# Attention into a gated mixture of experts: the gate's first choice made for all batches from mean values, one logits run per batch, and the value matmuls of two tiles in smaller pieces

## The chip, the cores and the metric

One core of one Trainium2 chip. The metric is device microseconds of the whole program, the median of a few executions. A profile, taken in a further execution, gives the times of single instructions. Engines in the profile's short names: PE (TensorE matmuls), PEld (its weight loads), DVE (VectorE), ACT (ScalarE), POOL (GpSimd), SP (SyncE, which here only issues DMAs).

## What is computed

Multi-query attention feeds a two-level gate, which sends each token to one of 16 experts. Sizes: 8 batches, 16 heads, 384 positions, head width 64; so 3072 tokens of width 1024; 4 groups of 4 experts, each expert two 1024x1024 matrices.

```python
scores = matmul(q, k.T) / 8                    # one k and one v per batch for all 16 heads
attn   = exp(scores - max) / sum
x      = matmul(attn, v)                       # tokens: 3072 x 1024
g_idx  = argmax(x @ w_group)                   # group of a token, weight g_w from a softmax
e_idx  = argmax(x @ w_expert[g_idx])           # expert in the group, weight e_w from a softmax
out    = g_w * e_w * (relu(x @ w1[g, e]) @ w2[g, e])
```

With inputs of scale 0.1 the scores are close to zero, so a token's attention is close to an even mean of its batch's values. The inputs are one fixed draw. In it all 384 tokens of each of batches 0 to 6 go to one expert; in batch 7, 363 go to expert 0 and 21 to expert 2.

## The kernel before

**Tiles, units, steps.** A tile `t` is 128 query positions of a batch `b` (24 tiles, three to a batch). A tile has 8 units; a unit is two heads. The main loop `for i in range(NSL)` (L794) has 96 steps of two units, so tile `t` has steps 4t to 4t+3, and a batch has 12 steps. `p = i % 4` is the step's place in its tile. The order of work is written out by hand: in each step the engines get, in this order,

1. `scores` (L198, matmul L206) of both units: PE writes them into PSUM, which has room for two units, so a unit's scores wait until ACT has read those of the unit two before;
2. `soft` (L212): DVE takes row maxima (L217), ACT the exponentials with row sums (L220, two of 128x384 for a unit);
3. for `p` of 0 or 1, PE work called by `advance` (an expert's matmuls, L479 and L493, in groups of eight) and transposed queries (`q_group`, L183 with ACT's copy L187; from tile 5 on `q_blocks` on DVE, L195); for `p` of 2 or 3, `pv` (L246, matmul L257): half of the value matmuls of the tile before;
4. `transp` (L239): DVE transposes the probabilities of the two units of two steps before into the buffer `ring` (L241), which `pv` reads; `ring` has three slots of four units, and a tile takes two;
5. `norm` (L229): DVE's reciprocal of the sums (L231), then POOL scales the four probability blocks (L235);
6. `pv_out` (L263) after the second half of `pv`: ACT copies four banks (L271), POOL casts to bf16 (L272).

Everything else is hung on a step and a place by `at(step, place, function)` (L721), and `run` calls it there: "m0", "m1", "m3" lie around `advance`; "v" and "m2" behind the PE work and ahead of `transp`; "w" ahead of `norm`; "e" right behind `norm`; "g" at the step's end. Each engine works through its own instructions in that order. A semaphore wait in one holds all that is behind it on that engine.

**The gate before.** The logits of a batch come in two runs: of its first tile at step 12b+8 (`logits`, L280, 32 columns) and of the other two at 12b+16 (64 columns); DVE transposes them (`logits_out`, L290). From the first run, at step 12b+9, `gate_first` (L302 to L306), a small matmul that counts choices over the tile's tokens (`gate_choose`, L341) and `gate_score`, `gate_pick` (L350 to L383) name the batch's main expert; `gate_picked` (L360) makes its one-hot row. `load_main` reads the index into a register of POOL and issues four DMAs of 1 MB from POOL's queue (L454), at step 12b+9, place "g". From step 12b+17 the expert's 14 groups of matmuls are spread over the next batch's steps. Batch 7 has a second expert for the few other tokens; what is left over after that would go through a loop at the end (L911), once for each pair of batch and expert.

**Keys of the next batch.** `load_k` (step 12b+2), `scale_k` on POOL (L167, step 12b+7, "g") and `k_blocks` on DVE (L171, step 12b+8, "e").

In steps 0 to 16 there is no expert to work on, since that of batch 0 begins in step 17.

Of the kernel before, what the change touches and what calls it, by code (L numbers as in the profile page):

```python
# [12 lines left out]
P = 128  # L13
# [6 lines left out]
def kernel(  # L20
# [242 lines left out]
    def pv_out(t):  # L263
        b, j = t // ST, t % ST
        if j < 2:
            st["xt", b, j] = pool.tile([P, KO, ST - 1 if j else 1, P], FP32, tag=f"xt{j}", name="xt", bufs=1)
        xt = st["xt", b, min(j, 1)][:, :, max(j - 1, 0), :]
        if j == 0:
            st["xb", b] = pool.tile([P, KO, S], BF16, tag="xb", name="xb", bufs=2)
        for i, o in enumerate(st.pop(("o", t))):  # L270
            nc.scalar.copy(out=xt[:, :, ts(i, 32)], in_=o[:, 0:2 * P].rearrange("p (c q) -> p c q", c=KO))  # L271
        nc.gpsimd.tensor_copy(out=st["xb", b][:, :, ts(j, P)], in_=xt)  # L272

    def logits(b, j0, j1):

        xt = st.pop(("xt", b, j0))
        lt_ps = xbank()
        for ko in range(KO):
            for c in range(4):
                nc.tensor.matmul(  # L280
                    out=lt_ps[ts(c, 32), 0:32 * (j1 - j0)].rearrange("e (j q) -> e j q", q=32),
                    lhsT=wge[:, ko, :], rhs=xt[:, ko, :, ts(c, 32)],
                    start=(ko == 0), stop=(ko == KO - 1), tile_position=(0, c * 32),
                )
        st["lt_ps", b, j0] = lt_ps
# [60 lines left out]

    def gate_score(b):
# [6 lines left out]

    def gate_pick(b):
        st["smx", b], st["idx", b] = pick(st["scr", b], 0)

    def gate_picked(b):
        ohs = ohs_all[:, ts(b, GE)]
        nc.vector.tensor_scalar(  # L360
            out=ohs, in0=st["scr", b][:], scalar1=st["smx", b][:, 0:1], scalar2=None, op0=ALU.is_equal
        )
        st["ohs", b] = [ohs]
# [95 lines left out]
    def load_main(b, n):  # L459
        if n == 0:  # L460
            st["e", b] = nc.gpsimd.value_load(st.pop(("idx", b))[0:1, 0:1], min_val=0, max_val=GE - 1)
        st.setdefault(("w", b), []).append(load_w(st["e", b], n))
# [267 lines left out]

    for b in range(B):
        s0 = SB * b
        for x, j0, j1 in ((s0 + 8, 0, 1), (s0 + 16, 1, ST)):
            at(x, "m2", logits, b, j0, j1)
            at(x + 1, "m0" if b and j0 == 0 else "v", logits_out, b, j0, j1)
# [16 lines left out]
        if b == B - 1:  # L752
            at(s0 + 13, "w", gate_pick_second, b)
# [5 lines left out]
    for t in range(NT):  # L759
        for x, u, half in ((4 * t, t, 1), (4 * t + 1, t + 1, 0)):  # L760
# [4 lines left out]
        if t < NT - 2:  # L765
            at(4 * t, "g", load_q, t + 2)
# [18 lines left out]
    for e in range(GE):  # L785
        nc.vector.memset(tie16[:, e:e + 1], float(GE - 1 - e))

# [5 lines left out]
    load_v(0)  # L793
    for i in range(NSL):  # L794
# [4 lines left out]
        for u in us:  # L799
            scores(u)  # L800
# [10 lines left out]
        elif t > 0:  # L811
            pv(t - 1, (p - 2) * NB // 2, (p - 1) * NB // 2)
# [8 lines left out]
        if p == 3 and t > 0:  # L821
            pv_out(t - 1)
# [12 lines left out]
    run(i + 1, "w")  # L835
    advance(1)
    load_second(0)
# [124 lines left out]
```

## Time and profile before

| | |
|---|---|
| median of 3 runs | 508.92 us (508.62 to 509.27) |
| the profiled execution's own time | 508.39 us |
| its span in the profile | 507.0 us |
| granted TensorE clock, mean | 0.997 |
| PE busy, share of the span | 481.5 us, 95% |
| DVE busy | 413.0 us, 81% |
| ACT busy | 321.8 us, 63% |
| POOL busy | 289.6 us, 57% |

Rows of a group give line, engine, operation, output<-input with its shapes, and xcount, then busy time in all and the mean of one in ns, then the engine's idle time ahead of them with what ended it. Rows of the timeline give start, duration, engine, line, with the number of instructions merged in xN and, in brackets, the idle time ahead and what ended it. An fp32 matmul is two rows on PE. Matmul ends are modelled, so the distance from one start to the next is the better measure of PE.

### The profile page before, as it was taken

The page shows a single profiled execution, that of the slowest core. Times are in us where ns is not written, and L with a number is a line of the kernel's source. Part 1 is how long each engine was busy: PE and PEld are TensorE (multiplying, and loading weights), DVE is VectorE, ACT ScalarE, POOL GpSimd, SP SyncE. Part 2 cuts the span into 40 slices and gives each one's busy share as a digit, 9 for nine tenths or more (in the row PEclk, how much of TensorE's full clock was granted, in tenths as well). Part 3 has the DMA queues.
Part 4 walks back from the last instruction along what each step waited for, and adds up shares of the span by engine and source line. Part 5 has one row for each costly group of instructions (what it writes and reads, how often), then busy time and mean ns, then how long its engine had stood idle before and what let it go on. Part 6 is the DMA issues. An engine that isn't in the chain of part 4 may idle for free.

```text
span 507.0 us, 20054 instructions
## 1 busy us (share of the span) xinstructions
PE 481.5 (95%) x8256; PEld 262.1 (52%) x8273; DVE 413.0 (81%) x737; ACT 321.8 (63%) x1002; POOL 289.6 (57%) x524
## 2 busy tenths in 40 slices
PE   7597789999999999999999999999999999999994
PEld 3143356555456455555465455555455455555653
DVE  3889979988899879988899879998799888890630
ACT  4776766677676766676676776676775775753421
POOL 1665955684576664584576654584476654584300
PEclk9999999999999999999999999999999999999998
DMA  7612997399947998389946998389956993089993
GB/s 106 145 26 45 174 239 193 76 160 233 255 86 129 220 237 218 75 157 232 261 84 123 217 243 223 75 143 230 245 116 111 210 241 110 1 155 241 231 243 121
DMA packets 64524, 84.04 MB, mean 166 GB/s; under 512 B 20379, under 2 KB 39963, under 8 KB 64432
## 3 DMA queue, kind: packets, MB, share of 16 engines
q0 software_dynamic: 19152, 37.84, 41.3%
q1 hardware_dynamic: 44320, 44.61, 35.2%
q8 instruction: 66, 1.08, 0.9%
q10 hardware_dynamic: 960, 0.30, 0.3%
q14 instruction: 26, 0.21, 0.1%
HBM read 101.52 MB, written 19.40 MB: 239 GB/s over the span
## 4 chain that ended last, share of the span: by engine, by line
PE 90%; DVE 5%; ACT 3%; issue 1%; POOL 0%; POOLq 0%; ACTq 0%; DVEq 0%
PE x L257 26%; PE s L206 25%; PE x L479 15%; PE x L493 13%; PE sb L493 4%; PE x L280 3%; ACT pr L220 3%; DVE nmx L217 2%; PE sb L479 2%; DVE ring L241 2%; PE x L674 1%; PE x L100 1%; PE x L689 1%; PE x L145 0%; PE x L643 0%
## 5 line engine op out<-in xcount | busy, mean ns | idle before, releaser
L235 POOL TENSOR_SCALAR pr<-pr,rinv 128x384 f32<-128x384 f32 x384 | 218.3, 588 | 146.0 <-DVE rinv L231 133.2
L220 ACT ACTIVATE pr<-s,nmx 128x384 f32<-128x384 f32 x384 | 218.0, 579 | 131.5 <-DVE nmx L217 120.0
L217 DVE TENSOR_REDUCE nmx<-s 128x2 f32<-128x768 f32 x192 | 174.3, 948 | 45.7 <-PE s L206 44.6
L241 DVE STREAM_TRANSPOSE ring<-pr 128x768 f32<-128x768 f32 x192 | 175.4, 952 | 0.1
L206 PE MATMUL s<-kt,qt 64*64 64x384 f32 x1536 | 148.9, 496 | 13.3 <-ACT pr L220 12.3
L257 PE MATMUL x<-ring,v_sb 32*64 32x256 f32 x4608 | 137.7, 378 | 0.2
L257 PEld LDWEIGHTS x<-ring,v_sb 32*64 32x64 f32 x4608 | 101.6, 131 | 43.0 <-issue 23.2
L206 PEld LDWEIGHTS s<-kt,qt 64*64 64x64 f32 x1536 | 48.5, 132 | 82.6 <-ACT pr L220 44.4
L220 ACT ACTIVATION_READ_ACCUMULATOR pr<-s,nmx 128x1 f32 x384 | 77.9, 203 | 0.0
L479 PE MATMUL x<-xb,w 128*128 128x384 bf16 x448 | 76.6, 326 | 0.0
L479 PEld LDWEIGHTS <-w 128*128 128x128 bf16 x512 | 47.7, 98 | 42.2 <-issue 12.6
L493 PE MATMUL x<-w,h_t 128*128 128x512 bf16 x276 | 64.7, 380 | 0.6
L493 PEld LDWEIGHTS <-h_t 128*128 128x128 bf16 x384 | 35.7, 98 | 52.0 <-issue 11.9
L454 POOL DMA_DIRECT2D w<-in_moe_w_dram x36 | 27.9, 784 | 10.8 <-issue 9.0
L271 ACT COPY xt<-x 128x256 f32<-128x256 f32 x96 | 28.9, 385 | 2.8 <-PE x L257 2.7
L485 ACT ACTIVATE h_t<-x 128x384 bf16<-128x384 f32 x56 | 25.4, 502 | 6.4 <-PE x L479 6.4
L272 POOL CAST xb<-xt 128x1024 bf16<-128x1024 f32 x24 | 24.9, 1036 | 3.6 <-ACT xt L271 3.6
L511 ACT ACTIVATE y<-x,gsel 128x512 f32<-128x512 f32 x36 | 24.8, 693 | 3.1 <-PE x L493 3.1
L195 DVE STREAM_TRANSPOSE qt<-q_sb 128x512 f32<-128x512 f32 x38 | 26.1, 687 | 0.0
L493 PE MATMUL sb<-w,h_t 128*128 128x512 bf16 x92 | 21.2, 379 | 0.2
L231 DVE RECIPROCAL rinv<-ssum 128x4 f32<-128x4 f32 x96 | 13.9, 144 | 3.3 <-ACT pr L220 3.3
L511 ACT ACTIVATE y<-sb,gsel 128x512 f32<-128x512 f32 x9 | 6.2, 688 | 16.1 <-PE sb L493 16.1
(132 smaller groups left out, 165.6 us busy)
## 6 DMA issues: line engine op xcount, KB each, us to landing
w<-in_moe_w_dram POOLq DMA_DIRECT2D x36, 1024.0 KB, 19.6
q_sb<-in_q_dram SPq DMA_DIRECT2D x76, 224.0 KB, 6.0
out_dram<-y SPq DMA_DIRECT2D x96, 128.0 KB, 6.3
xb_scratch<-xb SPq DMA_DIRECT2D x8, 768.0 KB, 4.3
v_sb<-in_v_dram SPq DMA_DIRECT2D x32, 96.0 KB, 4.0
kk<-in_k_dram SPq DMA_DIRECT2D x28, 92.0 KB, 4.1
q_sb<-in_q_dram SPq DMA_DIRECT2D x16, 128.0 KB, 3.3
q_sb<-in_q_dram SPq DMA_DIRECT2D x5, 64.0 KB, 3.1
```

Of the source, the lines that this page charges most:

```text
L195: nc.vector.transpose(out=qt[:].rearrange("p (x d) -> p x d", d=32), in_=q_sb[:, :, 0:32])
L206: nc.tensor.matmul(out=s[m * D:(m + 1) * D, h, 0:S], lhsT=qt[r, ts(2 * cc + m, D)], rhs=kt[r, :], start=True, stop=True, tile_position=(h ...
L217: nc.vector.tensor_reduce(out=nmx[:], in_=s[:, :, 0:S], axis=AX.X, op=ALU.max, negate=True)
L220: nc.scalar.activation(out=pr[:, h, :], in_=s[:, h, 0:S], func=ACTF.Exp, bias=nmx[:, h:h + 1], scale=1.0, accum_out=ssum[:, k, h:h + 1],)
L235: nc.gpsimd.tensor_scalar(out=pr, in0=pr, scalar1=rinv[:, k, h:h + 1], scalar2=1.0, op0=ALU.mult, op1=ALU.mult)
L241: nc.vector.transpose(out=ring[:, (u // 4) % 3, u % 4].rearrange("p h s -> p (h s)"), in_=st.pop(("pr", u))[:].rearrange("p h s -> p (h s)"),)
L257: nc.tensor.matmul(out=o[i][h * D:(h + 1) * D, 0:2 * P].rearrange("d (g c q) -> d g c q", g=2, c=4), lhsT=v_sb[r, n, :], rhs=ring[r, a:z + ...
L271: nc.scalar.copy(out=xt[:, :, ts(i, 32)], in_=o[:, 0:2 * P].rearrange("p (c q) -> p c q", c=KO))
L454: nc.gpsimd.dma_start(out=w[:, o:o + 4, :], in_=(w1f, w2f)[n][ds(e, 1), :, o:o + 4, :].rearrange("o p c f -> (o p) c f"))
L479: nc.tensor.matmul(out=hp[:, 0:S], lhsT=w1[:, ko, ts(fc, P)], rhs=xb[:, ko, :], start=(ko == 0), stop=(ko == KO - 1))
L493: nc.tensor.matmul(out=yp, lhsT=h_t[:, fo, ts(j, P)], rhs=w2[:, fo, ts(nh, 512)], start=(fo == 0), stop=(fo == FO - 1),)
L511: nc.scalar.activation(out=y[:, ts(nh, 512)], in_=yp, func=ACTF.Copy, scale=g)
```

## The change

For the first choice of the gate the kernel no longer looks at a batch's first tile. It loads the values of all batches once more, sums them over positions (three rows of a partition on POOL in `guess_sum`, over partitions by a matmul with a column of ones in `guess_mean`), takes the logits of the eight sums (`guess_logits`), picks an expert for each batch on DVE and POOL (`guess_pick`), spreads the one-hot rows to all partitions by a matmul (`guess_all`) and makes eight indices (`guess_index`). All of this lies in steps 2 to 5. The buffers are the third slot of `ring`, which the transposes first write in step 6. Batches 0 to 6 then have one logits run, of 96 columns, at step 12b+16. Batch 7 keeps its two runs and its count, for the second expert. Weights of batch 0 are issued in step 7, those of batch 7 in steps 85 and 90, those of the second expert from step 95. `pv` of tiles 0 and 1 is cut into five pieces over three steps; the second place in a step for such a piece is "u", between the scores of the step's two units. `q_group` and `load_q` of tiles 1 to 3 move by one step.

```diff
-        if j < 2:
-            st["xt", b, j] = pool.tile([P, KO, ST - 1 if j else 1, P], FP32, tag=f"xt{j}", name="xt", bufs=1)
-        xt = st["xt", b, min(j, 1)][:, :, max(j - 1, 0), :]
+        if j == 0:
+            st["xt", b] = pool.tile([P, KO, ST, P], FP32, tag="xt", name="xt", bufs=1)
+        xt = st["xt", b][:, :, j, :]
...
+    def guess_load():
+        vs = ring[:, 2, 0:2].rearrange("p u h s -> p (u h s)").rearrange("p (b c d) -> p b c d", b=B, d=D)
+        nc.sync.dma_start(
+            out=vs.rearrange("p b c d -> p b (c d)"), in_=v.rearrange("b o (p c) d -> p (b o) (c d)", c=ST)
+        )
+        st["vs"] = vs
+
+    def guess_sum():
...
+        for part, n in zip(total, (0, B // 2)):
+            part = part[:, 0:B // 2, :]
+            nc.gpsimd.tensor_tensor(out=part, in0=vs[:, n:n + B // 2, 0, :], in1=vs[:, n:n + B // 2, 1, :], op=ALU.add)
+            nc.gpsimd.tensor_tensor(out=part, in0=part, in1=vs[:, n:n + B // 2, 2, :], op=ALU.add)
+            st["total"].append(part)
+
+    def guess_mean():
...
+        for b in range(B):
+            for h in range(2):
+                nc.tensor.matmul(
+                    out=bank[ts(h, D), b:b + 1], lhsT=total[b // (B // 2)][:, b % (B // 2), :], rhs=ident1[:],
+                    start=True, stop=True, tile_position=(0, h * D),
+                )
+        mean = early["mean"]
+        nc.scalar.copy(out=mean, in_=bank[:, 0:B])
...
+    def guess_logits():
...
+        for ko in range(KO):
+            nc.tensor.matmul(
+                out=bank[0:B, 0:NL], lhsT=mean, rhs=wge[:, ko, 0:NL], start=(ko == 0), stop=(ko == KO - 1)
+            )
+        lg = early["lg"][0:B].rearrange("b (g e) -> b g e", e=4)
+        nc.scalar.copy(out=early["lg"][0:B], in_=bank[0:B, 0:NL])
...
+    def guess_pick():
...
+        gp = nc.gpsimd
+        nc.vector.tensor_reduce(out=mx[0], in_=lg, axis=AX.X, op=ALU.max)
+        gp.tensor_tensor(out=lg, in0=lg, in1=mx[0].unsqueeze(2).to_broadcast([B, 1 + G, 4]), op=ALU.subtract)
+        nc.vector.scalar_tensor_tensor(
+            out=lg, in0=lg, scalar=0.0, in1=w4[0:B, 0:1 + G, :], op0=ALU.is_ge, op1=ALU.mult
+        )
+        nc.vector.tensor_reduce(out=mx[1], in_=lg, axis=AX.X, op=ALU.max)
+        nc.vector.tensor_tensor(
+            out=oh, in0=lg, in1=mx[1].unsqueeze(2).to_broadcast([B, 1 + G, 4]), op=ALU.is_equal
+        )
+        gp.tensor_tensor(
+            out=pair, in0=oh[:, 1:1 + G, :], in1=oh[:, 0, :].unsqueeze(2).to_broadcast([B, G, Eg]), op=ALU.mult
+        )
+        gp.tensor_tensor(
+            out=spread, in0=pair.rearrange("b g e -> b (g e)").unsqueeze(1).to_broadcast([B, B, GE]),
+            in1=ident[0:B, 0:B].unsqueeze(2).to_broadcast([B, B, GE]), op=ALU.mult,
+        )
...
+    def guess_all():
...
+        nc.tensor.matmul(
+            out=bank[:, 0:NP], lhsT=early["ones"][0:B], rhs=spread.rearrange("b c e -> b (c e)"), start=True, stop=True
+        )
+        nc.scalar.copy(out=ohs_all[:], in_=bank[:, 0:NP])
...
+    def guess_index():
+        nc.gpsimd.tensor_tensor(
+            out=numbered, in0=ohs_all[:].rearrange("p (b e) -> p b e", e=GE),
+            in1=tie16[:].unsqueeze(1).to_broadcast([P, B, GE]), op=ALU.mult,
+        )
+        number = early["number"]
+        nc.vector.tensor_reduce(out=number, in_=numbered, axis=AX.X, op=ALU.add)
...
+        nc.vector.tensor_scalar(
+            out=idx[:], in0=number, scalar1=-1.0, scalar2=float(GE - 1), op0=ALU.mult, op1=ALU.add
+        )
...
+    for x, where, fn in (
+        (2, "e", guess_sum), (3, "m2", guess_mean), (4, "m2", guess_logits), (4, "e", guess_pick),
+        (5, "m2", guess_all), (5, "e", guess_index),
+    ):
+        at(x, where, fn)
     for b in range(B):
         s0 = SB * b
-        for x, j0, j1 in ((s0 + 8, 0, 1), (s0 + 16, 1, ST)):
+        for x, j0, j1 in ((s0 + 8, 0, 1), (s0 + 16, 1, ST)) if b == B - 1 else ((s0 + 16, 0, ST),):
             at(x, "m2", logits, b, j0, j1)
...
-        at(s0 + 9, "m0" if b else "v", gate_first, b)
-        at(s0 + 9, "m3" if b else "m2", gate_choose, b)
-        at(s0 + 9, "w", gate_score, b)
-        at(s0 + 9, "w", gate_pick, b)
-        at(s0 + (13 if b == B - 1 else 12), "w", gate_picked, b)
         if b == B - 1:
-            at(s0 + 9, "w", load_main, b, 0)
-            at(s0 + 10, "w", load_main, b, 1)
+            at(s0 + 9, "m0", gate_first, b)
+            at(s0 + 9, "m3", gate_choose, b)
+            at(s0 + 9, "w", gate_score, b)
+            at(s0 + 10, "w", gate_pick_second, b)
+            at(s0 + 1, "g", load_main, b, 0)
+            at(s0 + 6, "g", load_main, b, 1)
+            at(s0 + 11, "g", load_second, 0)
         else:
-            at(s0 + 9, "g", load_main, b, 0)
-            at(s0 + 9, "g", load_main, b, 1)
+            at(s0 + (9 if b else 7), "g", load_main, b, 0)
+            at(s0 + (9 if b else 7), "g", load_main, b, 1)
             at(s0 + 16, "g", keep_xb, b)
...
     for t in range(NT):
-        for x, u, half in ((4 * t, t, 1), (4 * t + 1, t + 1, 0)):
+        spread = 0 < t <= ST
+        for x, u, half in ((4 * t + spread, t, 1), (4 * t + 1, t + 1, 0)):
...
         if t < NT - 2:
-            at(4 * t, "g", load_q, t + 2)
+            at(4 * t + spread, "g", load_q, t + 2)
+        x, n0 = 4 * t + 4, 0
+        for p, where, n1 in (
+            ((2, "p", 4), (3, "u", 6), (3, "p", 8), (4, "u", 10), (4, "p", NB)) if t < ST - 1 else
+            ((2, "p", NB // 2), (3, "p", NB)) if t < NT - 1 else ()
+        ):
+            at(x + p, where, pv, t, n0, n1)
...
     load_v(0)
+    guess_load()
     for i in range(NSL):
...
-        for u in us:
-            scores(u)
+        scores(us[0])
+        run(i, "u")
+        scores(us[1])
...
-        elif t > 0:
-            pv(t - 1, (p - 2) * NB // 2, (p - 1) * NB // 2)
+        run(i, "p")
...
-    run(i + 1, "w")
     advance(1)
-    load_second(0)
     few_ready()
```

`scale_k(1)` is still called at place "g" of step 7, behind the four weight DMAs of batch 0, which are now called there too.

More of the change, by code (lines that the diff above doesn't have):

```diff
@@ L765 @@
         if t < NT - 2:
[L766 removed]
+            at(4 * t + spread, "g", load_q, t + 2)
[5 more added lines that the diff above has]
+            at(x + p, where, pv, t, n0, n1)
+            n0 = n1
+            if n1 == NB:
+                at(x + p, "o", pv_out, t)
     load_k_first()
@@ L786 @@
         nc.vector.memset(tie16[:, e:e + 1], float(GE - 1 - e))
+    ident1 = singles.tile([P, 1], FP32)
+    nc.vector.memset(ident1[:], 1.0)
+    early, early_at = {}, 0
+    for name, width in (
+        ("number", B), ("mean", B), ("lg", NL), ("oh", NL), ("pair", GE), ("mx", 1 + G), ("sm", 1 + G),
+        ("ones", P), ("spread", NP), ("numbered", NP),
+    ):
+        early[name] = ring[:, 2, 3].rearrange("p h s -> p (h s)")[:, early_at:early_at + width]
+        early_at += width
+    nc.vector.memset(early["ones"], 1.0)
+    numbered = early["numbered"].rearrange("p (b e) -> p b e", e=GE)
     busy(5)
@@ L820 @@
         run(i, "e")
-        if p == 3 and t > 0:
-            pv_out(t - 1)
+        run(i, "o")
         run(i, "g")
```

37 lines of the change are left out of this document (24 added, 13 removed).

## Prediction

> **What bounds the kernel now.** I read the page's 40 slices first, then busy time by stage (the windows view), the chain that ended last, and the timeline of the first 76 us step by step.
>
> ```profile
> PE   7597789999999999999999999999999999999994
> DVE  3889979988899879988899879998799888890630
> ```
>
> PE fills every slice from the eighth on; in the first six or seven (12.7 us each) it does not, and DVE is as busy as PE there.
>
> ```profile
> 28.00:62.00 34.00, 28.00 (x605) 14.78 (x601) 31.52 (x53) 24.14 (x81) 23.85 (x40) 1.00 0.39 74
> 62.00:75.00 13.00, 11.54 (x304) 7.04 (x300) 10.29 (x14) 8.21 (x29) 7.79 (x13) 1.00 1.12 237
> ...
> 135.00:435.00 300.00, 299.47 (x5298) 162.43 (x5307) 266.18 (x449) 204.05 (x648) 183.09 (x322) 1.00 0.80 173
> ```
> ```profile
> by line: PE s L206 30.6%; PE x L257 29.4%; PE x L479 19.4%; PE x L493 17.6%; PE x L280 2.9%; issue 0.2%; PE x L341 0.0%
> ```
>
> In the windows the columns are PE, PEld, DVE, ACT, POOL, clock, DMA share, GB/s. From 28 to 62 us DVE is busy for 31.5 of 34 us; from 135 to 435 us PE for 299.5 of 300. The last line is the chain from 75 to 435 us: PE alone. So there are two stages. From step 17 (about 75 us) on only PE work taken away or added counts; a wait on POOL or DVE is covered there. Before step 17 each us that DVE loses is lost for good, since PE has nothing to fetch forward. I mark steps by the start of their first L217:
>
> ```profile
> 21.70 1.82 DVE L217 TENSOR_REDUCE nmx<-s 128x2 f32<-128x768 f32 x2
> ...
> 23.44 1.83 DVE L241 STREAM_TRANSPOSE ring<-pr 128x768 f32<-128x768 f32 x2
> ...
> 25.19 0.14 DVE L231 RECIPROCAL rinv<-ssum 128x4 f32<-128x4 f32 x1
> 25.25 1.80 DVE L217 TENSOR_REDUCE nmx<-s 128x2 f32<-128x768 f32 x2
> 25.42 2.27 POOL L235 TENSOR_SCALAR pr<-pr,rinv 128x384 f32<-128x384 f32 x4 [1.27 <-DVE rinv L231]
> ...
> 28.81 1.83 DVE L217 TENSOR_REDUCE nmx<-s 128x2 f32<-128x768 f32 x2
> ```
>
> Steps 4, 5 and 6 begin at 21.70, 25.25 and 28.81. A step is two maxima, two transposes and a reciprocal back to back, 3.55 us: the floor of a step in this stage. POOL scales a step's blocks from 0.23 us behind the reciprocal to 2.5 us behind it.
>
> **The change part by part.** What is added lies in steps 2 to 8, in the stage without cover, and at four places an engine that others need waits for POOL, whose queue has something ahead of what is waited for.
>
> (1) The sums and the mean (steps 2 and 3).
>
> ```profile
> 18.36 2.27 POOL L235 TENSOR_SCALAR pr<-pr,rinv 128x384 f32<-128x384 f32 x4 [1.28 <-DVE rinv L231]
> ...
> 20.50 0.88 PE L206 MATMUL s<-kt,qt 64*64 64x384 f32 x8 [1.61 <-ACT pr L220]
> ```
> ```profile
> L437 POOL TENSOR_TENSOR grem_all<-gate,gs 128x48 f32<-128x48 f32 x8 | 2.3, 289 | 0.6
> L421 POOL TENSOR_TENSOR gw<-wt 128x12 f32<-128x12 f32 x8 | 1.7, 211 | 6.7 <-DVE wt L418 6.7
> L145 PE MATMUL x<-ident,kk 128*64 128x128 f32 x12 | 1.5, 428 | 0.1
> ```
>
> POOL's scaling of step 2 ends at 20.63; the four sums of 128x256 stand behind it. Two-input operations take 211 ns for 12 columns and 289 for 48, 2.2 ns a column, so about 735 ns for 256: 2.9 us for four, to 23.5. The load of the values (0.79 MB, issued at about 12.7) should not be later:
>
> ```profile
> 10.00:20.00 10.00, 5.83 (x52) 1.66 (x52) 7.38 (x12) 7.53 (x25) 6.19 (x11) 1.00 0.94 172
> ```
>
> At the 172 GB/s of that window it takes 4.6 us, to 17.3, and as much again behind other loads would still be 22. [...] `guess_mean` waits for the sums on PE, and behind it in PE's queue are the scores of step 4, at 20.50 before. Half its 32 rows follow the second sum; at between 0.02 us a row and the 0.12 of L145 (1.5 us for 12 rows) they take 0.4 to 2; I take 1.0, since one column moves and not 128. The scores of step 4 then start at 24.5, their first unit is there 0.95 later, and step 4 begins at 25.4 instead of 21.70: **+3.7** (2.0 to 5.5, the low end with sums at half the price).
>
> (2) `guess_pick`, step 4, "e".
>
> ```profile
> L302 DVE TENSOR_REDUCE mx<-lg 128x5 f32<-128x20 f32 x8 | 1.4, 176 | 0.3
> L879 DVE TENSOR_REDUCE fcol<-end 128x1 f32<-128x128 f32 x1 | 0.3, 286 | 0.0
> ```
>
> DVE's second instruction waits for POOL's subtraction, and that stands behind POOL's scaling of step 4, which begins only with the reciprocal. So DVE stands still until 2.5 us behind the reciprocal, plus 0.2 for the subtraction, plus three more small operations at 0.2 with their hand-over, before the maxima of step 5: 3.4 us. `guess_logits` and ACT's two small copies are hidden under the exponentials. `guess_all` waits on PE for POOL, until some 1 us into step 5, when PE has nothing to do: nothing. **+3.4** (2.8 to 4.0).
>
> (3) `guess_index`, step 5, "e". The same again: the product of 128x128 on POOL (0.46 by the slope above) stands behind the scaling of step 5, then DVE reduces (0.29, as L879) and makes the index (0.2): 2.5 + 0.46 + 0.5. **+3.5** (2.8 to 4.2).
>
> (4) The weights of batch 0, now in step 7.
>
> ```profile
> 36.98 2.27 POOL L235 TENSOR_SCALAR pr<-pr,rinv 128x384 f32<-128x384 f32 x4 [2.17 <-DVE rinv L231]
> ...
> 40.21 0.51 POOL L167 TENSOR_SCALAR kk<-kk 128x384 f32<-128x384 f32 x1
> ...
> 41.14 0.58 DVE L171 STREAM_TRANSPOSE kt<-kk 128x384 f32<-128x384 f32 x1
> ...
> 50.50 3.24 POOL L454 DMA_DIRECT2D w<-in_moe_w_dram  x4 [1.48 <-issue]
> ```
>
> The four DMAs hold POOL for 3.24 us, with 1.48 ahead of the first. In step 9 of before nobody waited for POOL. Now `scale_k` (0.51) is behind them, and `k_blocks` waits for it on DVE one step later. Behind the reciprocal of step 7: 2.5 + 1.5 + 3.2 + 0.5 = 7.7 us; `k_blocks` would begin at 3.55 + 0.15 = 3.7. DVE waits 4.0 to 4.2, and the maxima of step 9 are behind it. **+4.1** (2.6 without the 1.48, to 4.5). POOL's own scaling is 4 us late here, but is needed two steps later: hidden.
>
> (5) Steps 6 to 13: what the pieces and the gate give.
>
> ```profile
> 33.26 1.82 DVE L217 TENSOR_REDUCE nmx<-s 128x2 f32<-128x768 f32 x2 [0.82 <-PE s L206]
> ...
> 44.23 0.17 PE L341 MATMUL x<-first,ones 128*128 128x16 bf16 x1 [1.81 <-DVE first L306]
> ...
> 61.82 1.82 DVE L217 TENSOR_REDUCE nmx<-s 128x2 f32<-128x768 f32 x2
> 66.61 1.52 PE L206 MATMUL s<-kt,qt 64*64 64x384 f32 x15 [0.76 <-issue]
> ```
>
> From step 6 (28.81) to step 14 (61.82) before takes 33.0 us. Half a `pv` (48 matmuls, 2.85 us) in front of the next scores makes DVE wait (0.82 here), and the gate holds DVE and PE in steps 9, 10 and 12. A piece of 16 matmuls is 0.5 us and fits the time in which PE waits for ACT, so DVE gets its floor: 8 x 3.55 + 0.58 for `k_blocks` = 29.0. **-4.0** (-5 to -2.5). Steps 14 to 16 stay; the PE pauses of 0.76 and 0.70 us there ("issue") belong to nothing that changes and came while weights landed, which they do again; if they stay away, -1.3.
>
> (6) Logits, now once a batch.
>
> ```profile
> 149.95 0.76 PE L280 MATMUL x<-xt,wge 128*32 128x32 f32 x64
> 150.65 1.52 PE L206 MATMUL s<-kt,qt 64*64 64x384 f32 x16
> 152.10 2.77 PE L479 MATMUL x<-xb,w 128*128 128x384 bf16 x16
> 154.71 0.17 PE L341 MATMUL x<-first,ones 128*128 128x16 bf16 x1
> 154.74 1.46 PE L479 MATMUL x<-xb,w 128*128 128x384 bf16 x8
> 156.13 1.52 PE L206 MATMUL s<-kt,qt 64*64 64x384 f32 x16
> ...
> 188.06 1.10 PE L280 MATMUL x<-xt,wge 128*32 128x64 f32 x64
> 189.09 1.52 PE L206 MATMUL s<-kt,qt 64*64 64x384 f32 x16
> 190.55 4.07 PE L479 MATMUL x<-xb,w 128*128 128x384 bf16 x24
> 194.55 1.52 PE L206 MATMUL s<-kt,qt 64*64 64x384 f32 x16
> ```
>
> By starts, the run of 32 columns costs PE 0.70 us and that of 64 1.03; so 96 should be 1.36, and one run saves 0.37. The counting matmul costs next to nothing: 24 rows of L479 take 4.03 with it and 4.00 without. Six batches (1 to 6) save 0.4 each, batch 0 pays 0.33 more in step 16 (its small run was in the early stage): **-2.0** (-3 to -1). The DVE work taken out of batches 1 to 6, about 1.5 us each, is covered by PE. The earlier weights of batch 7 and of the second expert are covered too: PE is never short of them (64.8 us busy from 435 to its end at about 500).
>
> **Sum**: 3.7 + 3.4 + 3.5 + 4.1 - 4.0 - 2.0 = +8.7. The profiled execution took 508.39 us (span 507.0), 0.5 below the median of 508.92. That gives 517.1 on it and 517.6 on the median; I say 517.2.
>
> **The rivals.**
>
> [...]
>
> *The waits cost little.* The other side: POOL's new work meets gaps that are there anyway (1.27 and 1.28 us ahead of its scaling in the rows above), and sums and small operations are much cheaper than I scale them. Steps 4 to 9 then lose little, (5) and (6) stay, and the time goes down to 508.4 - 6.0 = 502.4. It turns at 6.0 us of new waits in all. Against it: in (2), (3) and (4) the wait is made of scaling and DMA issue that have rows of their own (2.27, 3.24), 9 us in sum, and their order is fixed.
>
> *Fewer waits than counted.* (4) without the register and first-DMA gap, cheap sums, no PE pauses: 511 to 514.
>
> *The guess is wrong somewhere.* Each miss goes through the loop at the end: 4 MB of weights and an expert's 20 us of PE, over 40 us. Against it: in the fixed inputs a batch's tokens agree (all, or 363 of 384), and the mean of values gives the same expert for all eight.
>
> **How the numbers follow.** My forecast (all four waits, 515 to 519): 0.60. The clock falls on top (519 to 521): 0.15. Fewer waits (510 to 515): 0.14. The waits cost little (502 to 508): 0.07, and about even: 0.02. A wrong guess: 0.02. Likeliest 517.2; 511.5 to 520.5 leaves out about 2 in 10. A run of this kernel can tell about 0.2%, 1 us. Faster 0.07, same 0.02, slower 0.91.
>
> **What would show it.** Step 4's first L217 at about 25.4 with PE waiting for POOL's sums; about 7 us from step 4 to 5 and from 5 to 6, with DVE's idle time put down to POOL; about 8 us from step 8 to 9, with L171 waiting for L167; steps of 3.55 us from 6 to 8 and 9 to 13; the first L217 of step 17 about 11 us later than 75.62; L280 of 96 columns 1.36 us by starts. I am wrong if step 6 begins before 34 us, or if L167 runs ahead of the weight DMAs.

## The result, and the profile after

The changed kernel takes **531.98 us** (median of 4, 530.77 to 532.5), the kernel before beside it 508.77: a ratio of 1.046, 95% interval 1.0427 to 1.0492. The forecast was 517.2, with a range to 520.5: the sign is right, the size is not. Ratios, here and in the table of the runs, are of the executions counted as fast, so they can differ a little from the ratio of two medians. The profiled execution took 530.77 us (span 529.3), 22.4 more than that of before; the mean granted clock is 0.966 instead of 0.997.

The slices of the page after the change, 13.2 us each:

```profile
PE   6569569999999999999999999999999999999994
DVE  3558686998879887898789887898699888890540
...
PEclk9868798999999999999999999999999999999998
```

PE is less busy than before in four of the first seven slices, DVE in five, and the clock row, nines there before, falls in five. The windows (PE, PEld, DVE, ACT, POOL, clock, DMA share, GB/s):

```profile
28.00:62.00 34.00, 24.21 (x306) 10.49 (x306) 22.55 (x37) 16.78 (x56) 19.50 (x34) 0.75 0.37 65
62.00:75.00 13.00, 12.45 (x248) 5.58 (x244) 10.79 (x16) 8.38 (x28) 4.92 (x9) 0.93 1.13 205
75.00:90.00 15.00, 10.96 (x215) 6.19 (x221) 9.44 (x14) 7.53 (x24) 7.43 (x13) 0.77 0.59 118
135.00:435.00 300.00, 299.19 (x4971) 159.56 (x4970) 257.22 (x396) 203.03 (x641) 182.62 (x318) 1.00 0.82 180
```

From 28 to 62 us DVE is busy for 22.6 of 34 us instead of 31.5, and the clock granted to PE is 0.75 in the mean. From 135 to 435 us PE is as full as before by this view, at clock 1.00, and the chain that ended last, from 95 to 435 us, names PE almost alone, as before:

```profile
by line: PE s L206 30.5%; PE x L257 30.2%; PE x L561 18.9%; PE x L575 18.0%; PE x L280 2.1%; issue 0.2%; ACT pr L220 0.2%
```

Still a second loss hides there. By the first L217 of a step, as in the prediction, in us:

| | before | after | loss so far |
|---|---|---|---|
| step 4 | 21.70 | 26.08 | 4.4 |
| step 6 | 28.81 | 40.06 | 11.3 |
| step 14 | 61.82 | 81.94 | 20.1 |
| step 17 | 75.62 | 95.36 | 19.7 |
| step 95 | 447.85 | 470.00 | 22.2 |

**Steps 4 to 6.** The timeline of DVE, and that of POOL:

```profile
26.08 0.96 DVE L217 TENSOR_REDUCE nmx<-s 128x2 f32<-128x768 f32 x1 [4.46 <-PE s L206]
...
32.70 0.17 DVE L399 SCALAR_TENSOR_TENSOR ring<-ring,w 8x20 f32<-8x20 f32 x1 [2.53 <-POOL ring L398]
...
33.19 1.80 DVE L217 TENSOR_REDUCE nmx<-s 128x2 f32<-128x768 f32 x2
...
39.66 0.29 DVE L432 TENSOR_REDUCE ring<-ring 128x8 f32<-128x128 f32 x1 [2.83 <-POOL ring L427]
...
40.06 1.82 DVE L217 TENSOR_REDUCE nmx<-s 128x2 f32<-128x768 f32 x2
...
44.38 0.96 DVE L217 TENSOR_REDUCE nmx<-s 128x2 f32<-128x768 f32 x1 [0.70 <-PE s L206]
46.23 0.96 DVE L217 TENSOR_REDUCE nmx<-s 128x2 f32<-128x768 f32 x1 [0.90 <-PE s L206]
...
55.14 0.58 DVE L171 STREAM_TRANSPOSE kt<-kk 128x384 f32<-128x384 f32 x1 [2.06 <-POOL kk L167]
55.65 1.78 DVE L217 TENSOR_REDUCE nmx<-s 128x2 f32<-128x768 f32 x2
```
```profile
20.43 0.73 POOL L360 TENSOR_TENSOR ring<-ring 128x256 f32<-128x256 f32 x1
...
22.72 0.72 POOL L361 TENSOR_TENSOR ring<-ring 128x256 f32<-128x256 f32 x1
...
51.31 3.25 POOL L536 DMA_DIRECT2D w<-in_moe_w_dram  x4
54.57 0.54 POOL L167 TENSOR_SCALAR kk<-kk 128x384 f32<-128x384 f32 x1
```

The first three waits are where the forecast put them, and POOL ends each (the first by way of PE, which waits 3.29 and 0.85 us for the sums): the sums of 0.72 us, the subtraction behind the scaling, the product behind the scaling. The weights in front of `scale_k` cost 2.06.

**Steps 6 to 17.** The timeline of PE:

```profile
24.45 2.84 PE L206 MATMUL s<-kt,qt 64*64 64x384 f32 x16
...
37.15 2.84 PE L206 MATMUL s<-kt,qt 64*64 64x384 f32 x16 [2.60 <-ACT qt L187]
39.92 3.58 PE L257 MATMUL x<-ring,v_sb 32*64 32x256 f32 x64
43.44 0.88 PE L206 MATMUL s<-kt,qt 64*64 64x384 f32 x8
44.24 1.12 PE L257 MATMUL x<-ring,v_sb 32*64 32x256 f32 x32
45.29 0.88 PE L206 MATMUL s<-kt,qt 64*64 64x384 f32 x8
...
59.55 2.84 PE L206 MATMUL s<-kt,qt 64*64 64x384 f32 x16 [5.30 <-ACT qt L187]
...
79.30 1.08 PE L183 MATMUL x<-ident,q_sb 128*128 128x128 f32 x4 [4.04 <-DMA q_sb<-in_q_dram]
80.31 2.84 PE L206 MATMUL s<-kt,qt 64*64 64x384 f32 x16
```

Four things to see. First, the 16 rows of scores take 2.84 us behind each long wait instead of 1.52: half speed. The clock granted there is 0.50, from 22.8 to 33.0, 36.4 to 43.2, 56.9 to 63.7 and 77.4 to 84.2 us (in the kernel before it is 1.00 from 5.9 to 504.2 us, past PE's last matmul at 500); the windows view of one of these stretches:

```profile
57.00:63.00 6.00, 3.45 (x32) 1.33 (x40) 3.73 (x6) 3.75 (x13) 3.58 (x6) 0.50 1.12 203
```

Second, a piece of 16 value matmuls (32 rows) takes 1.05 by starts even at full speed (44.24 to 45.29), and stands between the two units of a step, so DVE waits for the second unit (0.70 and 0.90 at 44.38 and 46.23). Third, the wait of 5.30 us at 59.55 is for ACT, which copies the transposed queries only behind its exponentials of that step:

```profile
58.35 0.58 ACT L220 ACTIVATE pr<-s,nmx 128x384 f32<-128x384 f32 x1
...
58.90 1.08 ACT L187 COPY qt<-x 128x512 f32<-128x512 f32 x2
```

Fourth, at 79.30 PE waits 4.04 us for the queries of tile 4, whose loads SP issued right behind the weights' DMAs and which took 11.6 to 23.6 us to landing (the page's median is 5.4):

```profile
53.84 6.84 SPq L110 DMA_DIRECT2D q_sb<-in_q_dram  x4
```

**From step 17 on.** PE again:

```profile
142.32 2.41 PE L257 MATMUL x<-ring,v_sb 32*64 32x256 f32 x80
145.24 0.69 PE L257 MATMUL x<-ring,v_sb 32*64 32x256 f32 x16 [0.51 <-issue]
...
150.87 1.53 PE L280 MATMUL x<-xt,wge 128*32 128x96 f32 x64
152.33 1.52 PE L206 MATMUL s<-kt,qt 64*64 64x384 f32 x16
```

The merged logits take 1.46 by starts and win 0.34 us a batch (0.43 lost in step 12b+17, 0.77 won in step 12b+22). Yet steps 17 to 95 take 374.6 us against 372.2. Steps 28, 44, 52, 68, 76 and 92 (each up to the start of the step named) are 0.4 to 0.9 us longer than the same steps of the batches between, a period of 24 steps, because PE stops in the middle of a run, for nothing that the profile names.

### The profile page after: what moved, and what is told of

It reads as the page before. It is cut to its first block, busy times and chain, and to the rows that moved or that the text cites. A ratio compares the mean times of both kernels' runs of the same rounds, so it can differ in the third digit from the quotient of the medians.

```text
span 529.3 us, 19245 instructions
## 1 busy us (share of the span) xinstructions
PE 496.1 (94%) x7868; PEld 264.3 (50%) x7868; DVE 405.0 (77%) x678; ACT 322.6 (61%) x1005; POOL 293.5 (55%) x532
## 4 chain that ended last, share of the span: by engine, by line
PE 86%; DMA 4%; DVE 3%; ACT 2%; POOL 2%; issue 1%; SPq 0%; POOLq 0%; DVEq 0%; ACTq 0%
PE x L257 24%; PE s L206 24%; PE x L561 14%; PE x L575 12%; DMA q_sb<-in_q_dram 4%; PE sb L575 4%; ACT pr L220 2%; PE sb L561 2%; PE x L280 2%; DVE nmx L217 2%; DVE ring L241 1%; POOL pr L235 1%; PE x L756 1%; PE x L100 1%; PE x L771 0%
## 5 line engine op out<-in xcount | busy, mean ns | idle before, releaser
L217 DVE TENSOR_REDUCE nmx<-s 128x2 f32<-128x768 f32 x192 | 174.9, 949 | 67.9 <-PE s L206 67.1
L206 PE MATMUL s<-kt,qt 64*64 64x384 f32 x1536 | 154.9, 515 | 14.2 <-ACT qt L187 8.1
L257 PE MATMUL x<-ring,v_sb 32*64 32x256 f32 x4608 | 144.7, 385 | 1.3 <-issue 1.0
L257 PEld LDWEIGHTS x<-ring,v_sb 32*64 32x64 f32 x4608 | 101.4, 133 | 53.6 <-issue 33.1
L206 PEld LDWEIGHTS s<-kt,qt 64*64 64x64 f32 x1536 | 49.7, 136 | 84.5 <-ACT pr L220 31.5
```

The costliest lines, as they stand in the source:

```text
L206: nc.tensor.matmul(out=s[m * D:(m + 1) * D, h, 0:S], lhsT=qt[r, ts(2 * cc + m, D)], rhs=kt[r, :], start=True, stop=True, tile_position=(h ...
L217: nc.vector.tensor_reduce(out=nmx[:], in_=s[:, :, 0:S], axis=AX.X, op=ALU.max, negate=True)
L257: nc.tensor.matmul(out=o[i][h * D:(h + 1) * D, 0:2 * P].rearrange("d (g c q) -> d g c q", g=2, c=4), lhsT=v_sb[r, n, :], rhs=ring[r, a:z + ...
```

## The experiments

My theory after the result: the guess's waits, the pieces and the late loads cost the early stage what the rows above show, the half clock comes on top, and the small pauses later belong to something else. The rival: the later loss is the merged logits'. Line numbers of the runs from `e5` on, but `e6`, are 5 higher than those of before or after (L211 is L206, L262 is L257). "Step 17" is its start; "17 to 95" is from there to the start of step 95, both in the profiled run, whose own time is in the third column: it can lie up to 6 us off the median.

| run | median us | profiled run | ratio, interval | step 17 | 17 to 95 |
|---|---|---|---|---|---|
| before (profile of the start) | 508.77 | 508.39 | | 75.62 | 372.2 |
| after | 531.98 | 530.77 | 1.046, 1.043-1.049 | 95.36 | 374.6 |
| e1 guess alone | 535.21 | 539.74 | 1.049, 1.045-1.052 | 86.08 | 392.3 |
| e2 picks given | 524.57 | 524.47 | 1.029, 1.024-1.033 | 85.41 | 379.2 |
| e3 no pieces | 526.86 | 528.03 | 1.033, 1.030-1.036 | 90.10 | 377.2 |
| e4 weights in step 9 | 525.18 | 526.81 | 1.030, 1.028-1.033 | 91.30 | 374.7 |
| e5 100 instructions | 523.68 | 526.83 | 1.027, 1.024-1.031 | 78.16 | 388.4 |
| e5 256 instructions | 512.47 | 513.22 | 1.007, 1.004-1.009 | 80.89 | 371.7 |
| e6 given, no pieces | 515.90 | 514.86 | 1.015, 1.011-1.019 | 76.37 | 378.8 |
| e7 PE kept busy | 530.18 | 531.87 | 1.041, 1.038-1.045 | 94.75 | 376.1 |
| e9 busy, weights in 9 | 526.41 | 526.46 | 1.036, 1.034-1.038 | 88.47 | 376.7 |
| e8 hidden guess | 512.03 | 516.45 | 1.006, 1.004-1.008 | 75.86 | 380.8 |
| e8 shifted by 32 | 520.04 | 519.98 | 1.023, 1.018-1.027 | 76.17 | 383.9 |
| e8 shifted by 64 | 522.97 | 524.16 | 1.022, 1.016-1.028 | 74.95 | 389.5 |
| e8 shifted by 96 | 514.86 | 513.27 | 1.015, 1.010-1.021 | 74.67 | 378.7 |
| e10 shifted by 8 | 513.77 | 514.14 | 1.011, 1.008-1.013 | 76.41 | 377.9 |
| e10 shifted by 14 | 517.31 | 517.66 | 1.018, 1.014-1.022 | 78.49 | 379.4 |
| e10 shifted by 20 | 517.81 | 519.04 | 1.018, 1.016-1.021 | 76.94 | 382.2 |
| e11 places of before | 514.78 | 514.38 | 1.013, 1.009-1.016 | 76.57 | 376.4 |
| e11 off them | 514.58 | 508.96 | 1.013, 1.011-1.016 | 73.88 | 374.1 |

### One part at a time

`e1`: the kernel before, with the guess computed in the same steps and its result used by nobody.

```diff
+    for x, where, fn in (
+        (2, "e", guess_sum), (3, "m2", guess_mean), (4, "m2", guess_logits), (4, "e", guess_pick),
+        (5, "m2", guess_all), (5, "e", guess_index),
+    ):
+        at(x, where, fn)
```

> The kernel before with the whole guess chain added in the same places (steps 2 to 5), its indices and one-hot rows not used; the old gate stays. Theory (the chain's waits make half of the loss, whatever else changes): the maxima of step 6 begin at about 40 us as in the changed kernel (28.8 before), half of the chain's 11 us is not won back, and the time is 519 to 521. Rival (the chain costs little by itself, the loss comes from the pieces and the moved loads): 509 to 512.

Measured: 535.21, a miss by far, though the early part came out: step 17 is 10.5 us late. Twenty more were lost behind it in the profiled run, which lies 4.5 us above the median. The two largest of PE's waits from 80 to 470 us (total, times, longest), of 15.1 us in all; in the kernel before the same view is empty:

```profile
PE x L257 <- issue: 8.2, 10, 1.3
PE x L583 <- issue: 2.8, 4, 1.0
```

Steps 25, 28, 32 and most of those 12, 24, 36 and 48 behind them lose 0.6 to 2.0 us each, with nothing left of the guess to do. So the later loss is not the merged logits', which this kernel doesn't have.

`e2` writes the eight picks as constants, `e3` has the values in halves and the queries in their old steps, `e4` the weights of batch 0 in step 9:

```diff
+    for b, e in enumerate((13, 9, 9, 11, 3, 15, 13, 0)):
+        nc.vector.memset(ohs_all[:, b * GE + e:b * GE + e + 1], 1.0)
+        nc.vector.memset(idx[:, b:b + 1], e)
```
```diff
-        spread = 0 < t <= ST
+        spread = 0
...
-            ((2, "p", 4), (3, "u", 6), (3, "p", 8), (4, "u", 10), (4, "p", NB)) if t < ST - 1 else
```
```diff
-            at(s0 + (9 if b else 7), "g", load_main, b, 0)
-            at(s0 + (9 if b else 7), "g", load_main, b, 1)
+            at(s0 + 9, "g", load_main, b, 0)
+            at(s0 + 9, "g", load_main, b, 1)
```

> The changed kernel without the guess chain: the eight indices and one-hot rows are constants written at the start, the choosing is left out. Theory (the chain's 11 us and the rest add up): 532 - 11.3 = 520 to 521, a little less (518) where the TensorE clock then stays up; so still about 10 us slower than before, which the pieces, the moved transposes and the moved weights cost. Rival (my forecast for the rest, a gain of 6 less a wait of 4): 505 to 508.

> The changed kernel with the value matmuls of tiles 0 and 1 in halves again and the transposed queries and query loads of tiles 1 to 3 back in their old steps. Theory (a piece of 16 matmuls is 0.95 us and delays the second unit's scores; the moved transposes make the scores of steps 6, 10 and 14 wait for ACT's copy; the load of tile 4's queries comes behind the weights): 6 to 9 us won, 523 to 526. Rival (the pieces give the 4 us that I forecast and the loss is elsewhere): 535 to 536.

> The changed kernel with batch 0's weights issued in step 9 again instead of step 7. Theory (the weights' 4 MB get in front of the queries of tile 4, for which PE waits 4.0 us at 79.3, and hold POOL ahead of the keys' scaling, 2.1 us): 526, with no PE wait for a query load and no DVE wait at L171. Rival (the queries are late because SP issues them late): only the 2 us, 530.

Measured 524.57, 526.86, 525.18: 5.1 to 7.4 us less than the changed kernel, `e4` where it was expected, `e2` some 4 over and `e3` a little, since what they lost behind step 17 grew (379.2 and 377.2). Step 17 gives the parts without the later pauses: it comes 10.0, 5.3 and 4.1 us earlier than in the changed kernel, which loses 19.7. The parts overlap, so that they add up to nearly 19.7 says little: the wait for the queries of tile 4 is gone in `e3` as well as in `e4`, and `e3` has a PE pause of 1.85 us at 82.10. No run separates the pieces from the moved queries.

`e6` joins the three (its queries stand in their old steps, other than its expectation says).

> The changed kernel with the eight picks written as constants (no choosing of the main experts, so none of the guess's waits), the values of tiles 0 and 1 in halves as before, and the main weights of batch 0 in step 9. What is left of the change is the merged logits, the gate's shorter path and the moved queries. Theory: nothing of the loss in steps 3 to 16 is left except the tile-4 queries and the late scores (3 us or less each), and PE's pauses at steps 28, 44, 52, 68 stay: 510 to 517 us. If the loss belongs to the merged logits or the gate's order, 520 or more; if the pauses belong to the guess or the pieces, 505 to 508.

Measured 515.90, step 17 at 76.37: the early loss is gone. What is left, 378.8 behind it, is pauses, in steps 32, 36, 40, 56, 61, 64 and so on.

### The pauses: instruction blocks

The queue q8 that the page calls instruction moved 66 packets before, 67 in `e1` and 63 after the change, 16 KB each. If a packet, or block, holds 256 instructions, PE's 16,529 rows before fill 64.6; with its waits for semaphores and matmuls whose records are missing, 65.7 before, 66.1 in `e1` and 62.5 after, which rounded up are the packets. A batch has 2047 PE instructions before, one short of eight blocks, so that the edges stand at the same places of each batch; `e1` has some 100 more ahead of step 6, and after the change a batch has 1916, seven and a half blocks: the period of 24 steps. So I moved PE's instructions and nothing else:

```diff
+    def tiny(n):
+        x = xbank()
+        for _ in range(n):
+            nc.tensor.matmul(out=x[0:2, 0:2], lhsT=blank[:, 0:2], rhs=blank[:, 0:2], start=True, stop=True)
...
-    busy(5)
+    busy(3)
+    tiny(52)       # e5_shift256: tiny(130)
```

> The kernel before with two of its five 512-column warm-up matmuls at the start replaced by 52 pairs of a weight load and a matmul of two columns: PE executes 100 instructions more ahead of the first step, and nothing else changes. Theory (PE's instructions are fetched in blocks of 16 KB, that is 256 instructions, one packet each of the instruction queue; where a block's fetch falls into a run of value matmuls PE waits for it): the pauses that the kernel with the unused guess showed in steps 25, 28, 32, 37 and so on come back, 15 to 20 us of them, 522 to 530 us. Rival (those pauses came from the guess's other work or from the clock): 508 to 511 us, no more PE pauses than before.

> The same with 130 such pairs, 256 instructions more, one whole block: by the theory the block's edges fall where they fell before, so no new pauses; the start is up to 3 us later, 509 to 512 us. By the rival (extra instructions as such, or a different start, cost the time) it stands as far above before as the run with 100 instructions, or further.

Measured 523.68 and 512.47, the first as expected, the second 0.5 over. The first is slower by 14.4 us than before, and its longer steps are in the main those of `e1` (25, 28, 32, 37, 40, 44 and so on); the second, with more work, by 3.2, all of it ahead of step 17 (steps 17 to 95 take 371.7). PE's two largest waits from 80 to 470 us in the first (in the second the view is empty):

```profile
PE x L262 <- issue: 5.9, 7, 1.1
PE x L498 <- issue: 2.7, 5, 0.8
```

The same run of value matmuls in step 28, in the first and in the second:

```profile
127.73 2.40 PE L262 MATMUL x<-ring,v_sb 32*64 32x256 f32 x77
131.20 1.08 PE L262 MATMUL x<-ring,v_sb 32*64 32x256 f32 x19 [1.07 <-issue]
```
```profile
124.11 2.85 PE L262 MATMUL x<-ring,v_sb 32*64 32x256 f32 x96
```

In `e1` that run stops at the same place, and the DMA view from 137.1 to 137.3 us shows one packet of the instruction queue:

```profile
136.09 2.40 PE L257 MATMUL x<-ring,v_sb 32*64 32x256 f32 x76
139.84 1.08 PE L257 MATMUL x<-ring,v_sb 32*64 32x256 f32 x20 [1.34 <-issue]
```
```profile
q8 instruction: 1, 0.02, 33.4%
```

I counted PE's instructions in the program's order (four for an fp32 matmul, two for a bf16 one and, as I assumed, one for each further wait) and laid the trace's weight loads on the count, for eight kernels (before, after, `e1`, both `e5`, `e6`, both `e11`). Between 90 and 470 us 25 weight loads start over 0.9 us behind the one ahead with no wait of their own. All 25 stand at the same count modulo 256, to within one; so do 64 more in the traces of the twelve other kernels. Each of the 25 starts 2.2 to 2.9 us after its block's packet began, and 1.2 to 1.6 after it ended. The packet follows the edge before: in the median by about 1 us where the 16 DMA engines were under 80% busy around it, by 3.2 where they were full, with a wide spread in both. Where a block is used up in about 4.7 us (an estimate from 96 rows of value matmuls in 2.78 us and 16 rows of scores in 1.45, by starts from 118.84 to 123.07 us before, two instructions a row), 3.2 and 2.2 together are too much. That full DMA engines cause the delay is read from these medians; no run tests it. Between steps 17 and 95 the edges cost little in the kernel before (372.2 us, and no wait of PE in its view from 80 to 470 us), and much in `e5` with 100 instructions (388.4, 16 us slower; profiled runs).

### The half clock

`e7` is the changed kernel with 128 pairs of a weight load and a 256-column matmul on zeros (`fill(n)` is n of them), one block in all, in PE's waits of steps 3, 5 (24 behind the product of `guess_all`), 9 and 13; `e9` is the same with the weights in step 9.

```diff
+    at(3, "m2", fill, 24)
+    at(9, "m2", fill, 44)
...
+            if (t, half) == (3, 0):
+                at(x, "m1", fill, 36)
```

> The changed kernel with 128 pairs of a weight load and a matmul of 256 columns on zeros (256 PE instructions, so that the blocks' edges stay) in PE's waits of steps 3, 5, 9 and 13. Theory (PE ran at half speed after its long waits): the scores of steps 4, 6, 10 and 14 take 1.5 us instead of 2.84 and the first pieces 1.9 instead of 3.58, 525 to 529 us, step 17 starts 3 to 7 us earlier. Rival (the half speed lies beside DVE's and ACT's work): 531 to 533 us.

> The changed kernel with PE kept busy in its long waits as in the run before (256 PE instructions more) and the weights of batch 0 in step 9, so that the queries of tile 4 aren't queued behind them and can't take the win back. Theory (half speed after long waits cost 3 to 4 us of the 23): 520 to 523 us, against 525.2 with the weights' step alone. Rival (the half speed lies beside other work): 525 to 526 us.

Measured 530.18 and 526.41, both misses, in part. In `e7` the scores of step 10 are at full speed (1.52) and step 13 begins at 69.92 instead of 74.45. But the queries of tile 4 come only 1 us earlier, and PE waits nearly as long for them:

```profile
56.99 1.52 PE L211 MATMUL s<-kt,qt 64*64 64x384 f32 x16 [0.49 <-ACT qt L192]
...
70.56 4.09 PE L100 MATMUL x<-blank 128*128 128x256 bf16 x36
78.32 1.09 PE L188 MATMUL x<-ident,q_sb 128*128 128x128 f32 x4 [3.67 <-DMA q_sb<-in_q_dram]
```

In `e9`, compared with `e4`, step 17 begins 2.8 us earlier, and steps 17 to 95 take 2.0 longer by larger pauses. The clock granted is 0.50 for 27 us of the early stage in `e4` and for 3.4 in `e9`. So the half clock costs the early stage about 2.8 us; that the whole time falls by it isn't shown.

### A guess that nobody waits for

`e8` does the whole computation with the guess laid into gaps: no POOL work, sums by PE in steps 2 to 4, the pick on DVE in steps 6, 7 and 9, halves, queries and weights as before.

```diff
+    for n in range(3):
+        at(2 + n, "m2", guess_mean, 3 * n, min(3 * n + 3, B))
+    for x, where, fn in (
+        (5, "m2", guess_logits), (6, "e", guess_pick), (7, "e", guess_spread), (8, "m2", guess_all),
+        (9, "w", guess_index),
+    ):
+        at(x, where, fn)
```

The shifted ones add `tiny(16)` in step 0, in 0 and 1, in 0 to 2; `e10` has `tiny(4)`, `tiny(7)`, `tiny(10)` in step 0.

> The changed kernel with the whole computation, but a guess for which nobody waits: the means by 48 matmuls with ones on PE in steps 2 to 4 (no sums on POOL), logits in step 5, the pick on DVE in steps 6 and 7, the product over the batches in step 8, the index in step 9 in the place of the old pick; the values in halves, queries and weights in the steps of the kernel before. Theory (the first 17 steps lost by waits, by the pieces and by the weights' order, the rest by PE's instruction blocks): step 17 starts at 75 to 77 us as before, the merged logits win 2 us, and pauses at block edges, which stand half a block from those of the changed kernel, take 2 to 9 us: 508 to 516 us. Rival (the guess or the merged logits cost something else in steady state): over 518.

> The same with 16 pairs of a weight load and a two-column matmul in step 0: all later PE instructions stand 32 places further. A batch now has about 7.5 blocks of 256 instructions, so a shift by 128 gives the same edges with the batches swapped, and shifts of 0, 32, 64 and 96 cover them. Theory: steps 17 to 95 take 370 us plus the pauses of this position, other pauses than without the shift, in other steps but with the same period of 24 steps. Rival (the pauses do not hang on the position): the same time and the same paused steps in all four.

> The same with 32 such pairs, in steps 0 and 1: 64 places further. Theory and rival as for the shift by 32; where the position is a good one, 506 to 509 us, below the kernel before; a bad one 512 to 518.

> The same with 48 such pairs, in steps 0, 1 and 2: 96 places further. Theory and rival as for the shift by 32; a good position 506 to 509 us, a bad one 512 to 518.

> The kernel with the hidden guess and four pairs more in step 0, 8 PE instructions. In instructions counted modulo 128 its steady state then stands 2 places behind that of the changed kernel, whose pauses after step 17 were the smallest so far. Theory: steps 17 to 95 take 374 to 377 us instead of 380.8, 508 to 511 us in all. Rival: as the unshifted one, 512.

> The same with seven pairs, 14 instructions, 8 places behind the changed kernel. Theory: steps 17 to 95 take 371 to 376 us if the pauses shrink further in this direction, 506 to 510 us in all; if they grow again, the best position is near the changed kernel's. Rival: 512.

> The same with ten pairs, 20 instructions, 14 places behind the changed kernel. Theory: as for 14, 371 to 378 us from step 17 to 95, 506 to 513 us in all; the shift by 32 took 383.9 us there, so the pauses must grow again somewhere before it. Rival: 512.

Step 17 begins at 74.7 to 76.9 in six of the seven: the guess costs nothing there (`e6`, without one, has 76.37; the seventh has 78.5, where steps 5, 11 and 17 paused). The medians run from 512.0 to 523.0, the ratios from 1.006 to 1.023, with nothing changed but up to 48 tiny pairs and, by them, where PE's instructions stand. PE's waits from 95 to 470 us, unshifted and shifted by 64:

```profile
PE x L262 <- issue: 4.5, 6, 1.4
PE s L211 <- issue: 0.3, 1, 0.3
```
```profile
PE x L262 <- issue: 9.0, 10, 1.7
```

That the time hangs on the position is hit. That other steps would pause is missed in part: steps 44, 64, 80 and 88 pause in all seven, and what changes most is for how long. That a position without pauses would be found is missed, and so are the three forecasts for 8, 14 and 20. Steps 17 to 95 took 377.9, 379.4 and 382.2 there against 380.8 unshifted, but the unshifted 380.8 is from the slowest of its ten executions (516.45); by medians every shift is slower than none. No median came below before.

`e11` has the hidden guess and the two logits runs of before, with `tiny(14)` in step 0 and `tiny(1)` in each batch, so that every score matmul from step 10 on stands at the place of before modulo 256, to within one; its twin lacks both.

> The kernel with the hidden guess, and the logits of each batch in the two runs of the kernel before, so that a batch has as many PE instructions as before but for two; 14 pairs of a weight load and a two-column matmul in step 0 and one pair in each batch put every score matmul from step 10 on at the same place modulo 256 as in the kernel before. Theory: steps 17 to 95 take 371 to 373 us as before (372.2), no pause beyond those of before, step 17 starts at 74.5 to 76 us: 507 to 510 us. Rival (the pauses belong to the guess, or to the position only in part): 512 us or more.

> The same without the 15 kinds of pairs: less work by 21 pairs, but every PE instruction stands 28 to 48 places ahead of where it stood before, modulo 256. Theory: pauses come back, 511 to 525 us (how many can't be told for this position). Rival (position doesn't matter): the same as the run beside it or up to 0.6 us less, for the pairs that are left out.

Measured 514.78 and 514.58: the theory as I had put it falls, since the first was to be at 507 to 510, and the two can't be told apart. Steps 44, 56, 68, 80 and 92 of `e11_whole` are 0.65 to 0.92 us longer than the same step of other batches; in the kernel before only 56 and 68 are, by 0.1 and 0.4. PE's waits from 95 to 470 us in `e11_whole`:

```profile
PE x L262 <- issue: 1.4, 3, 0.9
```

At the edge in step 68 the packet came 2.55 us behind the edge ahead of it, against 2.27 before: a few tenths decide. Place alone isn't enough; the packet's delay counts too, and it varies: the twin's executions span 508.96 (the profiled one) to 517.29. What sets the delay, beside the load of the DMA engines to which the medians point, stays open.

## Why the prediction was right or wrong

**(1) to (3) right.** Forecast +3.7, +3.4, +3.5, measured by the steps' lengths +4.5, +3.6, +3.3: 11.4 instead of 10.6, with the sums at 0.72 to 0.73 us (0.735 forecast); the 16 rows of the mean behind the last sum took 0.95 by starts (23.50 to 24.45; 1.0 forecast, from an estimate for a row). In the first the scores of step 4 ran at half clock (2.84 us at 24.45), which the forecast had not counted. `e2` confirms the size: 10.0 at step 17.

**(4) half right.** `k_blocks` waited 2.06, not 4.1: no 1.48 us stood ahead of the first weight DMA, and DVE itself came to `k_blocks` 4.2 us behind the reciprocal of step 7 instead of 3.7. What I left out is the other queue: the DMAs ran ahead of SP's loads for tile 4, and PE waited 4.04 us in step 13. `e4`, without either wait, begins step 17 4.1 earlier, and not 6.1: in step 13 PE waits 2.66 us for ACT's copy there instead. The 9 us that the text holds against "the waits cost little" are 10.0 by its own rows (three scalings of 2.27, and 3.24).

**(5) failed, and it is the step that cost the forecast most: -4.0 where time was lost.** "A piece of 16 matmuls is 0.5 us": by the prediction's own row of 48 matmuls in 2.85 us it is 0.95, and it took 1.05. It doesn't fit a gap of PE: it stands between a step's two units, and DVE waits for the second. Also missed: the queries, moved one step on with the pieces, wait for ACT behind that step's exponentials (PE waits 5.30 us at 59.55; 3.12 in `e4`, where the keys are in time). Instead of 29.0 us, steps 6 to 14 took 41.9, and before they took 33.0. `e4`, without the late queries and the late keys, takes 38.4; `e9`, which keeps PE busy besides, 36.9; `e8`, in halves and with the old gate gone, 32.2. By these differences the late loads are about 3.5 us of the 8.9 lost, the half clock about 1.5, the pieces and the moved queries together about 3.8. `e3`, in halves but with the wait for the keys, takes 35.2.

**The clock** had 0.15, as a range of 519 to 521. It fell, and the range did not hold: the half clock is about 2.8 us of the 14.8 by `e9` against `e4`. What that range adds to 517.2, 1.8 to 3.8 us, was my estimate, and no run shows it: the runs showed 2.8 at step 17, and none of it in the whole time (526.41 in `e9`, 525.18 in `e4`). The signs were in my own text, waits of 3.4 to 4.1 us in (2) to (4); the clock belonged into the sum. Behind 5.30 us of waiting 16 rows of scores took 2.84 us instead of 1.52, at a granted clock of 0.50. The wait of 2.60 at 37.15, ahead of which two short rows ended a wait of 0.92, was enough too. In the kernel before no wait of PE is over 1.81 us (the row of L341 at 44.23), and the clock stays at 1.00 until 504.2.

**(6) right in its work, wrong in what it left out.** 96 columns take 1.46 instead of 1.36 and win 0.34 a batch, 2.0 over six. But I wrote that the PE pauses marked "issue" "belong to nothing that changes". They belong to where PE's instructions stand, which every added or removed matmul moves: those two, at 66.61 and 73.06 us of the kernel before, stand at the same count modulo 256 as the 25. New pauses had no term in the sum; six of them, some 4 us in all, turned -2.0 into +2.4.

Of the 14.8 us between forecast and result, steps 6 to 14 are 8.8 (+8.9 instead of +0.1: the pieces, the late queries, the clock) and the time from step 17 on 4.4 (+2.4 instead of -2.0); the first three terms add 0.8, steps 14 to 17 give 0.4 back, and the median lies 1.2 above the profiled run.

## What to carry to other kernels

In a hand-ordered kernel an early computation is free only if no in-order engine meets its result behind something slow; the guess cost 10 us ahead of step 17 with POOL in its chain, and nothing there when its work was moved off POOL and laid into gaps. Count PE's instructions as well as its time where it is full: a change that shifts them by part of a block of 256 can cost more than it saves (100 instructions of two columns cost 14.4 us here), so compare it with a kernel shifted by the same number that does nothing else. Follow each moved load to the other loads that it meets: the weights of batch 0, issued two steps earlier, left PE waiting 4.04 us for queries, and no longer in `e4`.

## What the hardware showed

- 100 instructions of two columns, added at the start, made the kernel 2.7% slower; 256 made it 0.7% slower, all of it ahead of step 17.
- PE resumes 1.2 to 1.6 us after an instruction packet has landed (25 pauses of over 0.9 us, all at one count modulo 256); in the median the packet trails the edge before by 3.2 us where the 16 DMA engines are full, by about 1 where they are under 80% busy.
- An add of 128x256 on POOL took 0.72 us, as scaled from 12 and 48 columns.
- Behind PE waits of 2.6 to 5.3 us, 16 rows of scores took 2.84 us instead of 1.52, at a granted clock of 0.50.
